# Attention output summed with `o` as the moving operand and turned by VectorE, FFN weights w1 and w3 as moving operand: a decode kernel before and after

## The chip, the cores and the metric

The kernel runs on one core of one Trainium2 chip. The metric is the device time of one execution in microseconds (us). The profile's span is some 2 us shorter than the time (2.6 us in the kernel before), since it goes from the first to the last instruction. Ratios are the mean time of one kernel's fast runs over the mean of the other's fast runs of the same rounds, with a 95% interval, so they are not quite the ratio of the medians that stand beside them. In the profile lines PE is TensorE and PEld its weight loads, DVE is VectorE, ACT ScalarE, POOL GpSimd and SP the engine whose queue issues the loads.

## The reference, cut to what matters

One decode step of four sequences: layer norm of x, attention of 32 heads over the last 2048 positions of the cache, a SwiGLU FFN on the same normalised x, and the residual.

```python
# x: (4, 1, 640); k_cache, v_cache: (4, 32, 8192, 192); all bf16
xn = layernorm(x)
q = xn @ wq                                     # 32 heads of 192
k, v = k_cache[:, :, -2048:, :], v_cache[:, :, -2048:, :]
p = softmax(q @ k^T * 192 ** -0.5)
attn = (p @ v).reshape(B, 1, 32 * 192) @ wo
ffn = (silu(xn @ w1) * (xn @ w3)) @ w2          # 640 -> 1536 -> 640
return x + attn + ffn
```

K and V of the window are 3 MB each for every head, so 201 of the 223 MB that are loaded.

## The kernel before: what the change and the argument touch

A head's K and V each come in one transfer with one contiguous row of 24,576 bytes for each of the 128 partitions. The tile pools stand one behind another in a partition: constants first, then FFN weights, K (2 buffers), V (3), products, wo, small tiles.

```python
const = ctx.enter_context(tc.tile_pool(name="const", bufs=1))
fpool = ctx.enter_context(tc.tile_pool(name="ffn", bufs=1))
kpool = ctx.enter_context(tc.tile_pool(name="kt", bufs=KBUFS))
vpool = ctx.enter_context(tc.tile_pool(name="vt", bufs=VBUFS))
ppool = ctx.enter_context(tc.tile_pool(name="pr", bufs=PBUFS))
# ... wopool, small, PSUM pools ...

def load_k(h):
    kt = kpool.tile([P, NJ, Dh], BF16, tag="kt")
    nc.sync.dma_start(out=kt[:].rearrange("q j d -> q (j d)"),
                      in_=k_win[:, h].rearrange("b (p j) d -> p b (j d)", p=PB))
```

Scores: VectorE multiplies K with q (`mult`, four quarters a head), TensorE adds up groups of columns (`adder`), VectorE reduces. P·V leaves two halves (even and odd positions) in one PSUM tile. They are merged, turned and normalised head by head. (In `nc.tensor.matmul`, `lhsT` is called the stationary operand and `rhs` the moving one.)

```python
# pv(h), after its 32 matmuls: ScalarE masks the odd half
nc.scalar.activation(out=o_odd[:], in_=o_ps[:, Dh:2 * Dh], func=ACTF.Copy, scale=half[:, 1:2])
# pv_merge(h): VectorE adds the even half
nc.vector.scalar_tensor_tensor(out=o_raw[:], in0=o_banks[h % 2][:, 0:Dh], scalar=half[:, 0:1],
                               in1=o_odds.pop(h)[:], op0=ALU.mult, op1=ALU.add)
# ge_tr(h): six small matmuls with o as the stationary operand
for i in range(RPP):
    nc.tensor.matmul(gp[sl, i, :], lhsT=o_raw[:, i:Dh:RPP], rhs=sel[:], start=True, stop=True)
# ge_copy(h): times 1 / sum, into oT, which ge_proj multiplies with wo
# ffn_in: 60 matmuls a weight, each with a 128x128 block of it as the stationary operand
nc.tensor.matmul(ffn["ps"][:, c, :], lhsT=ffn[name][:, kc, c:F:FC], rhs=xnT[:, kc, 0, :], ...)
```

The loads run over one queue. The last ones are V of the last three heads, most of w2, the last wo, and two small pieces of w2.

## Time and profile before

| | before |
|---|---|
| time, median (range) of 3 runs | 530.63 us (529.79 to 531.39) |
| span of the profiled run | 527.5 us |
| load queue, share of 16 transfer engines | 98.7% |
| steady stretch, 60 to 480 us | 431 GB/s |
| VectorE / TensorE busy | 69% / 66% |

A reading of the page begins with the shares. Where the transfers are busy in every slice and no engine comes near that (69% at most here), an engine's busy time is not the bound. The next question is at which moments the transfers were *not* running at their rate. For that, busy time by stretch is the view. The lines themselves are in the prediction below.

### The profile page before, as it was taken

What the parts mean: (1) busy time and instruction counts of PE and PEld (TensorE: products, weight loads), DVE (VectorE), ACT (ScalarE), POOL (GpSimd) and SP (SyncE); (2) the same over time, 40 slices, a digit from 0 to 9 for tenths busy, and PEclk for the clock granted to TensorE, in tenths of its full rate; (3) what the DMA queues carried; (4) which work ended last, traced back from release to release, by engine and by line L of the source; (5) the groups of instructions that cost most, each with busy time, mean ns of one, the idle gap of its engine ahead of it and who ended that gap; (6) DMA issues with size and microseconds to landing.
All of it is one profiled execution on the core that took longest, in us unless ns stands there. A gap on an engine that the chain in (4) does not pass through costs nothing.

```text
span 527.5 us, 6169 instructions
## 1 busy us (share of the span) xinstructions
PE 350.7 (66%) x2642; PEld 163.0 (31%) x2643; DVE 362.9 (69%) x505; ACT 43.7 (8%) x144; POOL 1.1 (0%) x8
## 2 busy tenths in 40 slices
PE   2765866666856867666768765566676676656775
PEld 0322332332523433232323332232332332323333
DVE  3179885777558478686757887577768766777961
ACT  2111000000101000000000000000000000000010
POOL 0000000000000000000000000000000000000000
PEclk9989897988968797787887899799898977998987
DMA  8999999999999999999999999999999999999995
GB/s 358 432 432 415 418 439 436 421 442 422 430 440 425 434 426 435 432 432 432 432 431 432 430 429 436 426 436 428 430 435 429 435 429 435 429 434 419 434 429 216
DMA packets 11570, 223.35 MB, mean 423 GB/s; under 512 B 1292, under 2 KB 1304, under 8 KB 2584
## 3 DMA queue, kind: packets, MB, share of 16 engines
q1 hardware_dynamic: 11528, 222.96, 98.7%
q8 instruction: 20, 0.33, 0.2%
q14 instruction: 6, 0.05, 0.0%
q10 hardware_dynamic: 16, 0.01, 0.0%
HBM read 222.96 MB, written 0.01 MB: 423 GB/s over the span
## 4 chain that ended last, share of the span: by engine, by line
DMA 63%; DVE 20%; PE 13%; ACT 2%; issue 1%; SPq 0%
DMA kt<-in_A_k_cache_dram 49%; DVE pr L204 14%; PE ps L215 9%; DMA w<-in_B_w_dram 7%; DMA wo_t<-in_A_wo_dram 4%; DMA wt<-in_A_wq_dram 4%; DVE sc L223 3%; PE qps L172 1%; PE gp L301 1%; DVE z L259 1%; ACT ex L251 1%; PE mt L245 1%; PE o_ps L267 1%; ACT L251 0%; DVE o_raw L279 0%
## 5 line engine op out<-in xcount | busy, mean ns | idle before, releaser
L215 PE MATMUL ps<-pr,idb 128*128 128x512 bf16 x768 | 222.3, 433 | 152.6 <-DVE pr L204 152.4
L204 DVE TENSOR_TENSOR pr<-kt,qbc 128x3072 bf16<-128x3072 bf16 x128 | 224.0, 1751 | 102.0 <-DMA kt<-in_A_k_cache_dram 101.7
L215 PEld LDWEIGHTS <-idb 128*128 128x128 bf16 x768 | 78.5, 106 | 248.2 <-issue 195.6
L223 DVE TENSOR_REDUCE sc<-ps 128x16 f32<-128x512 f32 x128 | 87.4, 683 | 3.2 <-PE ps L215 2.2
L267 PE MATMUL o_ps<-vt,z 128*8 128x384 bf16 x1024 | 55.9, 355 | 1.4 <-DMA vt<-in_A_v_cache_dram 1.4
L267 PEld LDWEIGHTS <-z 128*8 128x8 bf16 x1024 | 25.2, 90 | 28.0 <-issue 17.0
L301 PEld LDWEIGHTS gp<-sel,o_raw 128*32 128x32 f32 x384 | 24.7, 151 | 16.4 <-issue 9.8
L274 ACT ACTIVATE o_odd<-o_ps,half 128x192 f32<-128x192 f32 x32 | 13.5, 421 | 189.4 <-PE o_ps L267 187.5
L301 PE MATMUL gp<-sel,o_raw 128*32 128x4 f32 x384 | 27.3, 200 | 0.8 <-DVE o_raw L279 0.8
L248 ACT COPY negm<-mt 128x1 f32<-128x1 f32 x32 | 5.1, 159 | 258.8 <-PE mt L245 258.8
L259 DVE TENSOR_TENSOR z<-ex,mask_b 128x256 bf16<-128x256 bf16 x32 | 13.5, 422 | 14.3 <-ACT ex L251 13.9
L172 PE MATMUL qps<-wt,xnT 128*128 128x512 bf16 x59 | 16.1, 429 | 5.3 <-DMA wt<-in_A_wq_dram 5.2
L279 DVE SCALAR_TENSOR_TENSOR o_raw<-o_ps,half,o_odd 128x192 f32<-128x192 f32 x32 | 13.1, 409 | 6.6 <-ACT o_odd L274 6.6
L178 DVE CAST qbc<-qps 128x512 bf16<-128x512 f32 x6 | 3.8, 685 | 18.2 <-PE qps L172 18.2
L245 PEld LDWEIGHTS mt<-ones_ff,gneg 1*128 1x128 f32 x64 | 10.2, 198 | 15.8 <-issue 14.4
L245 PE MATMUL mt<-ones_ff,gneg 1*128 1x1 f32 x64 | 12.9, 268 | 0.6 <-DVE gneg L240 0.6
L232 PE MATMUL mt<-idf,lmax 128*1 128x128 f32 x32 | 11.4, 357 | 1.1 <-DVE lmax L227 1.1
L251 ACT ACTIVATE ex<-sc,negm 128x64 bf16<-128x64 f32 x32 | 11.1, 348 | 1.0
L172 PEld LDWEIGHTS <-xnT 128*128 128x128 bf16 x60 | 6.4, 107 | 14.6 <-issue 8.7
L193 PE MATMUL acc<-wo_t,oT 128*4 128x320 bf16 x96 | 9.8, 308 | 0.4 <-DMA wo_t<-in_A_wo_dram 0.4
L237 DVE TENSOR_REDUCE gmax<-mt 1x4 f32<-1x128 f32 x32 | 8.8, 275 | 1.3 <-PE mt L232 0.8
L286 PEld LDWEIGHTS mt<-mask_f,rsum 128*32 128x32 f32 x64 | 4.6, 109 | 14.0 <-issue 12.5
(52 smaller groups left out, 84.2 us busy)
## 6 DMA issues: line engine op xcount, KB each, us to landing
kt<-in_A_k_cache_dram SPq DMA_DIRECT2D x32, 3072.0 KB, 19.8
vt<-in_A_v_cache_dram SPq DMA_DIRECT2D x32, 3072.0 KB, 27.4
wo_t<-in_A_wo_dram SPq DMA_DIRECT2D x8, 960.0 KB, 22.9
wt<-in_A_wq_dram SPq DMA_DIRECT2D x2, 3072.0 KB
w<-in_B_w_dram SPq DMA_DIRECT2D x2, 1920.0 KB, 24.3
wt<-in_A_wq_dram SPq DMA_DIRECT2D x1, 1536.0 KB, 19.9
w<-in_B_w_dram SPq DMA_DIRECT2D x1, 1280.0 KB, 34.9
w<-in_B_w_dram SPq DMA_DIRECT2D x2, 320.0 KB, 36.8
```

Of the source, the lines that this page charges most:

```text
L172: nc.tensor.matmul(qp[:], lhsT=xnT[:, kc].rearrange("p a b -> p (a b)"), rhs=wq_rows[kc][:, (c0 + i) * QC:(c0 + i + 1) * QC], start=(kc == ...
L204: nc.vector.tensor_tensor(out=pr[:], in0=kts[h][:, g * JQ:(g + 1) * JQ, :], in1=qbc[:, h * Dh:(h + 1) * Dh].unsqueeze(1).to_broadcast([P, ...
L215: nc.tensor.matmul(ps[:], lhsT=idb[:], rhs=pr[:, :, kk * DD:(kk + 1) * DD], start=(kk == 0), stop=(kk == NK - 1))
L223: nc.vector.tensor_reduce(out=scs[h][:, g * JQ:(g + 1) * JQ], in_=pss.pop(u)[:], axis=AX.X, op=ALU.add)
L232: nc.tensor.transpose(out=mt[0:1, 0:P], in_=chs[h][0][:], identity=idf[:])
L245: nc.tensor.matmul(mt[:, P:P + 1], lhsT=gneg[:].rearrange("o p b -> o (p b)"), rhs=ones_ff[0:1, 0:1], start=True, stop=True)
L251: nc.scalar.activation(out=ex[:], in_=scs.pop(h)[:], func=ACTF.Exp, bias=negm[:, 0:1], scale=SCALE, accum_out=rsum[:])
L259: nc.vector.tensor_tensor(out=z[:], in0=ex[:].unsqueeze(2).to_broadcast([P, NJ, B]), in1=mask_b[:].unsqueeze(1).to_broadcast([P, NJ, B]), ...
L267: nc.tensor.matmul(o_ps[c * CT:c * CT + 2 * B, :], lhsT=z[:, 2 * jj:2 * jj + 2, :], rhs=vt[:, 2 * jj:2 * jj + 2, :], start=(jj < 4), stop= ...
L274: nc.scalar.activation(out=o_odd[:], in_=o_ps[:, Dh:2 * Dh], func=ACTF.Copy, scale=half[:, 1:2])
L279: nc.vector.scalar_tensor_tensor(out=o_raw[:], in0=o_banks[h % 2][:, 0:Dh], scalar=half[:, 0:1], in1=o_odds.pop(h)[:], op0=ALU.mult, op1=A ...
L301: nc.tensor.matmul(gp[sl, i, :], lhsT=o_raw[:, i:Dh:RPP], rhs=sel[:], start=True, stop=True)
```

## The change

The intent is to take small instructions off TensorE and VectorE. `o` and the FFN weights w1 and w3 become the moving operand, and the normalising and the turn to columns are done once per four heads instead of once per head, with a VectorE transpose of 32x32 blocks. The residual is loaded a second time, later, so that its matmuls can come later; the final copy becomes one. The cut below leaves out that the FFN's product is now also turned on VectorE (one 128x384 pass into `hb` and one transpose), that the softmax sums land in `po`, and that the sums of heads 29 and 30 come one or two slots earlier.

```diff
-        nc.scalar.activation(out=o_odd[:], in_=o_ps[:, Dh:2 * Dh], func=ACTF.Copy, scale=half[:, 1:2])
+        o_sb = small.tile([P, 2 * Dh], FP32, tag="o_sb", bufs=2, name="o_sb")
+        nc.scalar.copy(out=o_sb[:], in_=o_ps[:])
 ...
-        nc.vector.scalar_tensor_tensor(out=o_raw[:], ...)          # pv_merge, every head
-        nc.vector.reciprocal(out=rtb[sl, :], ...)                   # ge_norm, every head
-        for i in range(RPP):                                        # ge_tr, every head
-            nc.tensor.matmul(gp[sl, i, :], lhsT=o_raw[:, i:Dh:RPP], rhs=sel[:], start=True, stop=True)
-        nc.vector.tensor_tensor(out=oTs[hg][sl], ...)               # ge_copy, every head
+        for par in range(2):                                        # ge_sum, every head
+            nc.tensor.matmul(po[sl, 0:Dh], lhsT=sel_w[:, par].rearrange("p a b -> p (a b)"),
+                             rhs=o_sb[:, par * Dh:(par + 1) * Dh], start=(par == 0), stop=(par == 1))
+        nc.vector.reciprocal(out=rt[:], in_=po[:, Dh:Dh + 1])       # ge_rec, every four heads
+        og = small.tile([P, RPP, CT], BF16, tag="og", bufs=1, name="og")   # ge_turn, every four heads
+        nc.vector.tensor_scalar_mul(out=og[:].rearrange("p i r -> p r i"),
+                                    in0=po[:, 0:Dh].rearrange("p (r i) -> p r i", i=RPP), scalar1=rts.pop(hg)[:, 0:1])
+        oT = small.tile([P, RPP, CT], BF16, tag="oT", bufs=2, name="oT")
+        nc.vector.transpose(out=oT[:].rearrange("p i r -> p (i r)"), in_=og[:].rearrange("p i r -> p (i r)"))
 ...
-    half, sel = const.tile([P, 2], FP32), const.tile([P, B], FP32)          # shortened
-    sT, hT = const.tile([P, FC, B], FP32), const.tile([P, FC, B], BF16)     # shortened
+    tot_w, sel_w = const.tile([P, NREP, B], FP32), const.tile([P, 2, NREP, B], FP32)   # shortened
+    sT = const.tile([P, FW], FP32, name="sT")
+    hb = const.tile([P, FC, CT], BF16, name="hb")
+    hT = const.tile([P, FC, CT], BF16, name="hT")
 ...
+        xr["t"] = const.tile([B, D], BF16, name="x_res")
+        nc.sync.dma_start(out=xr["t"][:], in_=A_x.rearrange("b s d -> (b s) d"))
 ...
-                nc.tensor.matmul(ffn["ps"][:, c, :], lhsT=ffn[name][:, kc, c:F:FC], rhs=xnT[:, kc, 0, :], ...)
+                nc.tensor.matmul(ffn["ps"][w * CT:(w + 1) * CT, :], lhsT=xnT[:, kc].rearrange("p a b -> p (a b)")[:, 0:CT],
+                                 rhs=ffn[name][:, kc, w * FW:(w + 1) * FW], ...)
 ...
-    nc.vector.tensor_copy(out=res[:, 0:NH], in_=acc[0:NR, 0:NH])
-    nc.scalar.copy(out=res[:, NH:N0], in_=acc[0:NR, NH:N0])
+    nc.vector.tensor_copy(out=res[:], in_=acc[0:NR, :])
```

More of the change, by code (lines that the diff above doesn't have):

```diff
@@ L64 @@
     assert JQ * DD == 512 and JQ % 2 == 0 and 2 * Dh <= 512 and 2 * N0 == D and N0 <= 512
-    assert (H * Dh) % QC == 0 and NQ % 6 == 0 and QW % P == 0 and Dh % RPP == 0 and P == HG * CT
+    assert (H * Dh) % QC == 0 and NQ % 6 == 0 and QW % P == 0 and Dh == CT * RPP and P == HG * CT and F == HG * CT * FC
     assert 2 * H * Dh <= NJ * Dh and KBUFS == 2 and VBUFS == 3
@@ L79 @@
     ps_t = ctx.enter_context(tc.tile_pool(name="ps_t", bufs=1, space=MemoryType.PSUM))
+    ps_po = ctx.enter_context(tc.tile_pool(name="ps_po", bufs=1, space=MemoryType.PSUM))
     ps_acc = ctx.enter_context(tc.tile_pool(name="ps_acc", bufs=1, space=MemoryType.PSUM))
@@ L85 @@
     kts, vts, prs, pss, scs, exs, zs = {}, {}, {}, {}, {}, {}, {}
-    wos, o_odds, o_raws, rsums, rtbs, chs, ges, oTs = {}, {}, {}, {}, {}, {}, {}, {}
+    wos, o_sbs, rsums, rts, chs, oTs = {}, {}, {}, {}, {}, {}
     def load_k(h):
@@ L132 @@
                             axis=AX.X, op=ALU.add)
-    half = const.tile([P, 2], FP32, name="half")
-    nc.vector.tensor_reduce(out=half[:], in_=rows[:].rearrange("q (two b) -> q two b", b=B), axis=AX.X, op=ALU.add)
-    sel = const.tile([P, B], FP32, name="sel")
-    nc.vector.tensor_tensor(out=sel[:], in0=rows[:, 0:B], in1=rows[:, B:2 * B], op=ALU.add)
+    NREP = CT // B
+    tot_w = const.tile([P, NREP, B], FP32, name="tot_w")
+    nc.vector.tensor_copy(out=tot_w[:], in_=mask_f[:].unsqueeze(1).to_broadcast([P, NREP, B]))
+    sel_w = const.tile([P, 2, NREP, B], FP32, name="sel_w")
+    for par in range(2):
+        nc.vector.tensor_copy(out=sel_w[:, par], in_=rows[:, par * B:(par + 1) * B].unsqueeze(1).to_broadcast([P, NREP, B]))
     xf = ppool.tile([B, D], FP32, tag="pr")
@@ L197, in acc_add, with x_load, x_add @@
             acc_half(i, lhsT, rhs, last=last)
-    acc_half(0, idb[0:B, 0:B], x_sb, first=True)
+    po = ps_po.tile([P, Dh + 1], FP32, name="po")
+    xr = {}
+    def x_load():
+        xr["t"] = const.tile([B, D], BF16, name="x_res")
+        nc.sync.dma_start(out=xr["t"][:], in_=A_x.rearrange("b s d -> (b s) d"))
+    def x_add(i):
+        acc_half(i, idb[0:B, 0:B], xr["t"], first=True)
     def mult(u):
@@ L230, in chain_tr @@
     def chain_tr(h):
-        mt = ps_m.tile([P, P + 1 + B], FP32, tag="mt")
+        mt = ps_m.tile([P, P + 1], FP32, tag="mt")
         nc.tensor.transpose(out=mt[0:1, 0:P], in_=chs[h][0][:], identity=idf[:])
@@ L272, in pv @@
         vts.pop(h)
-        o_odd = small.tile([P, Dh], FP32, tag="o_odd", bufs=2, name="o_odd")
-        nc.scalar.activation(out=o_odd[:], in_=o_ps[:, Dh:2 * Dh], func=ACTF.Copy, scale=half[:, 1:2])
-        o_odds[h] = o_odd
-    def pv_merge(h):
-        o_raw = small.tile([P, Dh], FP32, tag="o_raw", bufs=2, name="o_raw")
-        nc.vector.scalar_tensor_tensor(out=o_raw[:], in0=o_banks[h % 2][:, 0:Dh], scalar=half[:, 0:1],
-                                       in1=o_odds.pop(h)[:], op0=ALU.mult, op1=ALU.add)
-        o_raws[h] = o_raw
+        o_sb = small.tile([P, 2 * Dh], FP32, tag="o_sb", bufs=2, name="o_sb")
@@ L284, in ge_tot @@
+        nc.scalar.copy(out=o_sb[:], in_=o_ps[:])
+        o_sbs[h] = o_sb
     def ge_tot(h):
         sl = slice((h % HG) * CT, (h % HG + 1) * CT)
-        nc.tensor.matmul(chs[h][1][sl, P + 1:P + 1 + B], lhsT=rsums.pop(h)[:].to_broadcast([P, CT]), rhs=mask_f[:],
+        nc.tensor.matmul(po[sl, Dh:Dh + 1], lhsT=tot_w[:].rearrange("p a b -> p (a b)"), rhs=rsums.pop(h)[:],
                          start=True, stop=True)
-    def ge_norm(h):
-        sl = slice((h % HG) * CT, (h % HG + 1) * CT)
-        rtb = small.tile([P, B], FP32, tag="rtb")
-        nc.vector.reciprocal(out=rtb[sl, :], in_=chs.pop(h)[1][sl, P + 1:P + 1 + B])
-        rtbs[h] = rtb
@@ L295, in ge_tr @@
-    def ge_tr(h):
-        hl = h % HG
-        sl = slice(hl * CT, (hl + 1) * CT)
-        gp = ps_t.tile([P, RPP, B], FP32, tag="t", name="gp")
-        o_raw = o_raws.pop(h)
-        for i in range(RPP):
-            nc.tensor.matmul(gp[sl, i, :], lhsT=o_raw[:, i:Dh:RPP], rhs=sel[:], start=True, stop=True)
-        ges[h] = gp
-    def ge_copy(h):
-        hg, hl = h // HG, h % HG
-        sl = slice(hl * CT, (hl + 1) * CT)
-        if hl == 0:
-            oTs[hg] = small.tile([P, RPP, B], BF16, tag="oT", bufs=2, name="oT")
-        nc.vector.tensor_tensor(out=oTs[hg][sl], in0=ges.pop(h)[sl, :, :],
-                                in1=rtbs.pop(h)[sl, :].unsqueeze(1).to_broadcast([CT, RPP, B]), op=ALU.mult)
+        chs.pop(h)
@@ new lines, in ge_rec, with ge_sum @@
+    def ge_rec(hg):
+        rt = small.tile([P, 1], FP32, tag="rt", bufs=2, name="rt")
+        nc.vector.reciprocal(out=rt[:], in_=po[:, Dh:Dh + 1])
+        rts[hg] = rt
+    def ge_sum(h):
+        sl = slice((h % HG) * CT, (h % HG + 1) * CT)
+        o_sb = o_sbs.pop(h)
+        for par in range(2):
+            nc.tensor.matmul(po[sl, 0:Dh], lhsT=sel_w[:, par].rearrange("p a b -> p (a b)"),
+                             rhs=o_sb[:, par * Dh:(par + 1) * Dh], start=(par == 0), stop=(par == 1))
@@ L312, in ge_proj, with ge_turn @@
+    def ge_turn(hg):
+        og = small.tile([P, RPP, CT], BF16, tag="og", bufs=1, name="og")
[3 more added lines that the diff above has]
+        nc.vector.transpose(out=oT[:].rearrange("p i r -> p (i r)"), in_=og[:].rearrange("p i r -> p (i r)"))
+        oTs[hg] = oT
     def ge_proj(hg, i0, i1):
@@ L314, in ge_proj @@
         for i in range(i0, i1):
-            acc_add(oT[:, i, :], wo_t[:, i * D:(i + 1) * D])
-    sT = const.tile([P, FC, B], FP32, name="sT")
-    hT = const.tile([P, FC, B], BF16, name="hT")
+            acc_add(oT[:, i, 0:B], wo_t[:, i * D:(i + 1) * D])
+    FW = F // HG
+    sT = const.tile([P, FW], FP32, name="sT")
+    hb = const.tile([P, FC, CT], BF16, name="hb")
+    hT = const.tile([P, FC, CT], BF16, name="hT")
     ffn = {}
@@ L325, in ffn_load, with ffn_in @@
         ffn[name] = wt
-    def ffn_in(name, c0, c1):
-        if c0 == 0:
-            ffn["ps"] = ps_t.tile([P, FC, B], FP32, tag="t", name="f_ps")
-        for c in range(c0, c1):
-            for kc in range(KC):
-                nc.tensor.matmul(ffn["ps"][:, c, :], lhsT=ffn[name][:, kc, c:F:FC], rhs=xnT[:, kc, 0, :],
-                                 start=(kc == 0), stop=(kc == KC - 1))
+    def ffn_in(name):
+        ffn["ps"] = ps_t.tile([P, FW], FP32, tag="t", name="f_ps")
+        for kc in range(KC):
+            for w in range(HG):
+                nc.tensor.matmul(ffn["ps"][w * CT:(w + 1) * CT, :], lhsT=xnT[:, kc].rearrange("p a b -> p (a b)")[:, 0:CT],
+                                 rhs=ffn[name][:, kc, w * FW:(w + 1) * FW], start=(kc == 0), stop=(kc == KC - 1))
     def ffn_silu():
@@ L338, in ffn_h @@
     def ffn_h():
-        nc.vector.tensor_tensor(out=hT[:], in0=ffn.pop("ps")[:], in1=sT[:], op=ALU.mult)
+        nc.vector.tensor_tensor(out=hb[:].rearrange("p c r -> p r c"),
+                                in0=ffn.pop("ps")[:].rearrange("p (r c) -> p r c", c=FC),
+                                in1=sT[:].rearrange("p (r c) -> p r c", c=FC), op=ALU.mult)
+        nc.vector.transpose(out=hT[:].rearrange("p c r -> p (c r)"), in_=hb[:].rearrange("p c r -> p (c r)"))
     w2_v = B_w2.rearrange("(p c) n -> p c n", c=FC)
@@ L352, in ffn_out @@
         for c in range(*W2C[i:i + 2]):
-            acc_add(hT[:, c, :], ffn["w2"][:, c, :], last=(c == FC - 1))
+            acc_add(hT[:, c, 0:B], ffn["w2"][:, c, :], last=(c == FC - 1))
     sched = defaultdict(list)
@@ L358, in add @@
         sched[slot].append((phase, len(sched[slot]), fn, args))
-    ends = {H - 3: (NU - 1, NU + 3), H - 2: (NU + 2, NU + 4), H - 1: (NU + 6, NU + 7)}
+    ends = {H - 3: (NU - 1, NU + 1), H - 2: (NU + 2, NU + 3), H - 1: (NU + 6, NU + 7)}
     for h in range(H):
@@ L378 @@
         add(ul + 4, 5, ge_tot, h)
-        add(ul + 4, 9, ge_norm, h)
+        if h % HG == HG - 1:
+            add(ul + 4, 9, ge_rec, h // HG)
         v, m = ends.get(h, (u0 + L, u0 + L + 1))
         add(v, 7, pv, h)
-        add(m, 0, pv_merge, h)
-        add(m, 7, ge_tr, h)
-        add(m + 1, 0, ge_copy, h)
+        add(m, 7, ge_sum, h)
+        if h % HG == HG - 1:
+            add(m + 1, 0, ge_turn, h // HG)
     e = ends[H - 1][1] + 1
@@ L392 @@
     add(f, 0, ffn_load, "w1", B_w1)
-    add(f + 7, 7, ffn_in, "w1", 0, FC)
+    add(f + 7, 7, ffn_in, "w1")
     add(f + 7, 9, ffn_silu)
     add(f + 8, 0, ffn_load, "w3", B_w3)
-    add(f + 15, 7, ffn_in, "w3", 0, FC)
+    add(f + 15, 7, ffn_in, "w3")
     add(f + 15, 9, ffn_h)
-    add(1, 6, acc_half, 1, idb[0:B, 0:B], x_sb, True)
+    add(8, 0, x_load)
+    add(16, 6, x_add, 0)
+    add(17, 6, x_add, 1)
     add((H - 3) * GQ + 1, 0, wo_load, NG - 2)
@@ L417 @@
             fn(*args)
-    NR, NH = CT + B, N0 // 2
+    NR = CT + B
     res = ppool.tile([NR, N0], BF16, tag="pr", name="res")
-    nc.vector.tensor_copy(out=res[:, 0:NH], in_=acc[0:NR, 0:NH])
-    nc.scalar.copy(out=res[:, NH:N0], in_=acc[0:NR, NH:N0])
+    nc.vector.tensor_copy(out=res[:], in_=acc[0:NR, :])
     out_v = out.rearrange("b s d -> (b s) d")
```

## The prediction

> **What bounds the kernel now.** I read the busy line first, then the forty slices, then the queues and the share of the chain that ended last.
>
> ```profile
> PE 350.7 (66%) x2642; PEld 163.0 (31%) x2643; DVE 362.9 (69%) x505; ACT 43.7 (8%) x144; POOL 1.1 (0%) x8
> ...
> DMA  8999999999999999999999999999999999999995
> GB/s 358 432 432 415 418 439 436 421 442 422 430 440 425 434 426 435 432 432 432 432 431 432 430 429 436 426 436 428 430 435 429 435 429 435 429 434 419 434 429 216
> ...
> q1 hardware_dynamic: 11528, 222.96, 98.7%
> ...
> DMA 63%; DVE 20%; PE 13%; ACT 2%; issue 1%; SPq 0%
> ```
>
> No compute engine is above 69%, while the one load queue keeps the 16 transfer engines busy for 98.7% of the span, and every slice but the first and the last reads 9. The kernel is a stream of 222.96 MB, almost all K and V. The chain gives VectorE 20% and TensorE 13%, but the chain names what releases the next *issue* on the queue; it does not say that the engines moving data stood still. So I asked for busy time by stretch (columns: stretch and its length, busy time and count of each engine, clock, DMA share, GB/s):
>
> ```profile
> 2.00:524.00 522.00, 350.32 (x2640) 162.99 (x2643) 362.29 (x503) 42.80 (x143) 0.00 (x0) 0.88 1.00 427
> 5.00:510.00 505.00, 340.05 (x2502) 156.79 (x2503) 356.85 (x485) 40.61 (x137) 0.00 (x0) 0.88 1.00 431
> 520.00:524.00 4.00, 3.21 (x46) 2.17 (x47) 0.60 (x2) 0.30 (x1) 0.00 (x0) 0.84 0.38 154
> ...
> 42.00:44.00 2.00, 1.19 (x7) 0.48 (x5) 2.00 (x2) 0.00 (x0) 0.00 (x0) 1.00 0.86 258
> ```
>
> For 505 us the rate is 431 GB/s; the only hole I found is at 42 to 44 us (258 GB/s, so about 0.8 us lost at 430), where the queue waits for the first K buffer to come free. From about 485 us the queue waits for nothing: all last loads are issued by 488.2 us and need until 523.95. The end itself (columns: start, duration, what):
>
> ```profile
> 487.85 36.06 DMA w<-in_B_w_dram
> 523.90 0.04 issue
> 523.95 0.45 PE acc L193 x4
> 524.40 0.02 issue
> 524.42 0.33 DVE res L421
> 524.75 0.02 issue
> 524.77 0.29 ACT res L422
> ```
>
> The last piece of w2 lands, four matmuls and two copies follow, then the output goes out. Compute can shorten the time only before about 5 us, in the 0.8 us hole, or after 523.95.
>
> [...] this change adds 5 KB. [...] about 5 KB / 431 GB/s = 0.01 us. [...]
>
> **The change part by part.** These rows go (line, engine, operation, shapes, count, busy us, mean ns):
>
> ```profile
> L301 PE MATMUL gp<-sel,o_raw 128*32 128x4 f32 x384 | 27.3, 200 | 0.8 <-DVE o_raw L279 0.8
> L274 ACT ACTIVATE o_odd<-o_ps,half 128x192 f32<-128x192 f32 x32 | 13.5, 421 | 189.4 <-PE o_ps L267 187.5
> L279 DVE SCALAR_TENSOR_TENSOR o_raw<-o_ps,half,o_odd 128x192 f32<-128x192 f32 x32 | 13.1, 409 | 6.6 <-ACT o_odd L274 6.6
> L292 DVE RECIPROCAL rtb<-mt 32x4 f32<-32x4 f32 x32 | 5.6, 176 | 1.9 <-PE mt L286 1.2
> L309 DVE TENSOR_TENSOR oT<-gp,rtb 32x24 bf16<-32x24 f32 x32 | 5.6, 176 | 3.0 <-PE gp L301 2.7
> ```
>
> VectorE loses 13.1 + 5.6 + 5.6 = 24.3 us. It gains, once per four heads, a reciprocal (0.18), a normalising pass over 128x192 from PSUM (like o_raw, 0.41) and a 128x192 bf16 transpose[...]. Eight times 0.97 is 7.8 us. Net about -16.5 us, to 346 us.
> ScalarE copies 384 columns instead of 192. Slope from 421 ns at 192 to the 594 ns cast at 512: 0.54 ns a column, so 0.52 us, 32 times +0.1 = +3 us.
> TensorE: 12 records a head become four of 192 columns (an f32 matmul of this program is two records: 384 = 32 x 6 x 2). The 120 FFN matmuls of 4 columns, each with a 128x128 weight load, become 40 of 384 columns in four column groups. I expect 10 to 20 us less busy time, but leave this rough, since TensorE waits 152.4 us for the products anyway.
> All of it lies beside the transfers. In the steady stretch VectorE already sits idle 101.7 us for K; it will sit idle about 118. The hole at 42 us follows from the first four products, which the change does not touch; the load of x is issued later.
>
> The path that can move is **the tail**. Before: the last P·V ends at 519.8, the first w2 piece's 16 matmuls and the 12 small ones end near 522.05, oT is ready at 522.28, its projection starts at 522.43 with the last wo, and all is done at 524.40. After: the same 16 matmuls end near 521.8 (estimate); two f32 matmuls of 192 columns take 0.6 to 0.9 us (estimate from the 128-column f32 record's 270 ns against 200 ns for 4 columns, and a granted clock of 0.50 from 517 to 520); then 0.41 + 0.38 and two hand-overs of 0.05. So oT is ready near 523.5, 1.2 us later. The projection's 12 and the last 8 matmuls took 0.98 + about 0.5 us when ready, so the sums end near 525.1: +0.7. Then one 36x320 cast, 317 + 160 x 1.05 = 0.48 us, replaces 0.33 + 0.02 + 0.29: -0.15. **Sum: +0.55 us, so about 531.2 us** on the median of 530.63.
>
> **The rivals.** (a) *Faster because engines are relieved.* 16 us of VectorE and the small matmuls in the chain's list speak for it. [...] It could take at most the 0.8 us hole and some of the shortfall between 427 and 431: at best 528.5. (b) *The shared PSUM tile `po` becomes a wait.* The first head of each next group writes its sum into `po` after the old group is normalised. By the schedule, normalising stands in slot 22 and the next write to the tile in slot 23 (counted in quarter heads from the group's start), so the order fits; if it stalled TensorE, K has about 3.5 us of queued data (a head's 6.29 MB lasts 14.6 us, four products' slots take about 11). Nothing until then; at worst +3 us. (c) *The tail costs more,* if the clock stays at 0.50: the f32 pair doubles, +0.7 us more, 531.9. (d) *The residual's load is late* and holds TensorE: it is issued near 53 us, needed eight slots later, and loads land in about 23 us. I expect no wait.
>
> **Range and chances.** Three runs before lie between 529.79 and 531.39, so scatter is ±0.8 us. The tail gives 0 to +1.2, the stream perhaps -1 to +0.5. Central 531.1, range 529.6 to 532.6. 2% is 10.6 us: [...] a loss needs an unseen stall in each group. Same: 0.98.
>
> **What would show it right or wrong.** Right: slices of the transfers still 9, queue near 98.7%, VectorE near 346 us with its wait for K up by about 15 us, span within 2 us; last w2 landing near 524; oT after it or close to it; sums ending 0.3 to 1.2 us later after that landing than the 0.45 us here. Wrong: slices of 8 or less in the middle, a TensorE wait on the normalising, the transpose or x_res of more than 1 us each, or a transpose far above 0.4 us.

The 0.38 us for the transpose (part of the 0.97, and in 0.41 + 0.38) rests on no trace of this case; in the changed kernel it took 378 ns (L311 of its page). The 1.05 ns a column of the last cast is the slope, in the kernel before, between the 36x160 cast, 317 ns, and the 128x512 cast, 685 ns. That no rate above 431 GB/s can be had, as the 528.5 of rival (a) assumes, was not shown either: from 60 to 480 us these runs reach 431 or 432 at most.

## The result, and the profile after

The changed kernel takes 533.78 us (median of 4 runs, 532.4 to 534.3) against 530.39 (4 runs). The ratio is 1.0058 [1.0032, 1.0084], some 3.1 us longer: inside 2%, but above the predicted range.

The same lines of the page of the changed kernel (busy by engine, transfers in forty slices, the load queue, the chain):

```profile
PE 342.7 (65%) x2306; PEld 144.5 (27%) x2307; DVE 350.2 (66%) x435; ACT 45.6 (9%) x143; POOL 1.1 (0%) x8
...
DMA  8999999999999999999999999999999999999995
GB/s 356 445 417 422 417 435 434 426 434 422 431 434 421 433 423 433 430 426 433 426 423 437 424 428 429 428 432 424 428 429 432 427 432 426 432 427 406 428 427 220
...
q1 hardware_dynamic: 11536, 222.97, 98.6%
...
DMA 60%; DVE 23%; PE 15%; ACT 1%; issue 1%; SPq 0%
```

VectorE has 12.7 us less to do, TensorE 8 us less. The queue is as full as before (98.6%, the slices still read 9), with the same bytes. Yet 15 of the 40 slices read 430 or more, where 24 did before. The steady stretch says it in one number. First the kernel before, then the changed one (stretch, length, busy time and count of PE, weight loads, VectorE, ScalarE and GpSimd, clock, transfer share, GB/s):

```profile
60.00:480.00 420.00, 282.96 (x2175) 132.65 (x2173) 302.21 (x412) 30.95 (x114) 0.00 (x0) 0.87 1.00 431
```

```profile
60.00:480.00 420.00, 274.71 (x1866) 114.66 (x1865) 285.70 (x345) 31.59 (x108) 0.00 (x0) 0.88 1.00 429
```

The share is 1.00 in both: the transfer engines did not stand idle for a late buffer, so the pieces took a little longer. Over 420 us, 2 GB/s of 431 are about 2 us, and the whole stream is 520 us long. V of the last head, for which the last P·V waits, lands at 519.79 instead of 517.10 us, so 2.7 of the 3.0 us of span are lost before the tail begins.

The tail, in the chain that ended last of the changed kernel (start, duration, what):

```profile
524.34 1.08 DVE og L308
525.42 0.02 issue
525.44 0.39 DVE oT L311
525.83 0.04 issue
525.87 1.54 PE acc L196 x20
527.41 0.02 issue
527.44 0.48 DVE res L430
```

Nothing here waits for a transfer any more: the chain runs over the normalising pass and the transpose. From the moment at which the first w2 piece lets its matmuls begin to the issue of the output it is 522.91 to 527.95, 5.04 us; before, 520.15 to 525.09, 4.94 us. The tail costs 0.1 us in this pair of profiles.

The new groups that carry it (line, engine, operation, shapes, count, busy us, mean ns, idle before):

```profile
L303 PE MATMUL po<-o_sb,sel_w 128*32 128x192 f32 x128 | 35.0, 409 | 0.5 <-ACT o_sb L285 0.5
L285 ACT COPY o_sb<-o_ps 128x384 f32<-128x384 f32 x32 | 15.3, 479 | 193.6 <-PE o_ps L278 193.6
L308 DVE TENSOR_SCALAR og<-po,rt 128x192 bf16<-128x192 f32 x8 | 8.4, 1055 | 8.0 <-PE po L303 8.0
L311 DVE STREAM_TRANSPOSE oT<-og 128x192 bf16<-128x192 bf16 x8 | 3.0, 378 | 0.3
```

So two things called for a cause: a stream that is 0.5% slower with the same bytes and no gap, and a normalising pass of 1,055 ns where 410 were expected.

### The profile page after: what moved, and what is told of

Read it like the earlier page. It is cut to its first block, busy times and chain, and to the rows that moved or that the text cites.

```text
span 530.5 us, 5427 instructions
## 1 busy us (share of the span) xinstructions
PE 342.7 (65%) x2306; PEld 144.5 (27%) x2307; DVE 350.2 (66%) x435; ACT 45.6 (9%) x143; POOL 1.1 (0%) x8
## 3 DMA queue, kind: packets, MB, share of 16 engines
q1 hardware_dynamic: 11536, 222.97, 98.6%
## 4 chain that ended last, share of the span: by engine, by line
DMA 60%; DVE 23%; PE 15%; ACT 1%; issue 1%; SPq 0%
DMA kt<-in_A_k_cache_dram 50%; DVE pr L215 15%; PE ps L226 8%; DMA w<-in_B_w_dram 6%; DVE sc L234 4%; DMA wt<-in_A_wq_dram 3%; PE qps L175 2%; PE po L303 2%; DVE og L308 1%; DVE z L270 1%; PE o_ps L278 1%; ACT ex L262 1%; PE acc L196 1%; DVE oT L311 1%; ACT L262 0%
## 5 line engine op out<-in xcount | busy, mean ns | idle before, releaser
L226 PE MATMUL ps<-pr,idb 128*128 128x512 bf16 x768 | 212.5, 418 | 161.8 <-DVE pr L215 161.8
L215 DVE TENSOR_TENSOR pr<-kt,qbc 128x3072 bf16<-128x3072 bf16 x128 | 223.3, 1745 | 110.6 <-DMA kt<-in_A_k_cache_dram 110.6
L226 PEld LDWEIGHTS <-idb 128*128 128x128 bf16 x768 | 76.2, 103 | 262.8 <-issue 206.4
L303 PE MATMUL po<-o_sb,sel_w 128*32 128x192 f32 x128 | 35.0, 409 | 0.5 <-ACT o_sb L285 0.5
L285 ACT COPY o_sb<-o_ps 128x384 f32<-128x384 f32 x32 | 15.3, 479 | 193.6 <-PE o_ps L278 193.6
L303 PEld LDWEIGHTS po<-o_sb,sel_w 128*32 128x32 f32 x128 | 13.8, 130 | 20.9 <-issue 14.5
L308 DVE TENSOR_SCALAR og<-po,rt 128x192 bf16<-128x192 f32 x8 | 8.4, 1055 | 8.0 <-PE po L303 8.0
L290 PEld LDWEIGHTS po<-rsum,tot_w 128*32 128x32 f32 x64 | 4.7, 112 | 14.7 <-issue 13.1
```

Of the source, the lines that this page charges most:

```text
L215: nc.vector.tensor_tensor(out=pr[:], in0=kts[h][:, g * JQ:(g + 1) * JQ, :], in1=qbc[:, h * Dh:(h + 1) * Dh].unsqueeze(1).to_broadcast([P, ...
L226: nc.tensor.matmul(ps[:], lhsT=idb[:], rhs=pr[:, :, kk * DD:(kk + 1) * DD], start=(kk == 0), stop=(kk == NK - 1))
L285: nc.scalar.copy(out=o_sb[:], in_=o_ps[:])
L303: nc.tensor.matmul(po[sl, 0:Dh], lhsT=sel_w[:, par].rearrange("p a b -> p (a b)"), rhs=o_sb[:, par * Dh:(par + 1) * Dh], start=(par == 0), ...
L308: nc.vector.tensor_scalar_mul(out=og[:].rearrange("p i r -> p r i"), in0=po[:, 0:Dh].rearrange("p (r i) -> p r i", i=RPP), scalar1=rts.pop ...
```

## The experiments

**Where the buffers start.** The engines' work did not explain a slower transfer without a gap, so I read the placement of the buffers from the two built programs (bytes from the start of a partition):

```
                 constants end   first K buffer             first V buffer
before                  34,560   49,920  = 195 x 256         99,072 = 387 x 256
changed                 38,944   54,304  = 212 x 256 + 32   103,456 = 404 x 256 + 32
```

The constants of the changed kernel are 4,384 bytes larger: x_res 1,280, sT 1,344, hb 768, hT 672, and tot_w with sel_w in place of half with sel 320 (half and sel with 32 bytes each: only so do the parts add up to the 4,384). 4,384 is 17 x 256 + 32. Every big buffer begins 32 bytes past a multiple of 256. That is theory A. Theory B is the natural rival: wider f32 copies and f32 sums that get in the transfers' way. Theory C is the small load of x in the middle of the stream.

In what follows "steady" is the rate from 60 to 480 us. Each run had its own runs of the kernel before on the same chip: 529.89 us for the first four experiments, 530.57 for the next four, 529.76 for the last four.

### b_p288: only the placement of the changed kernel

```diff
     hT = const.tile([P, FC, B], BF16, name="hT")
+    pad = const.tile([P, 72], FP32, name="pad")     # never used
```

> The kernel before with one unused constant of 288 bytes a partition behind the others: no instruction changes, only where the big buffers start (K, V, weights: 0 bytes past a multiple of 64 before; 32 bytes past one here, as in the changed kernel). Theory A (the stream is slower because its destinations start off alignment): 2 to 3 us slower than before, rate in the steady stretch 428 to 429 GB/s instead of 431. Theory B (the stream is slower because of what the engines do beside it: wider f32 copies, the f32 sums): the time of before within 0.7 us, 431 GB/s.

Measured: 534.50 us against 529.89, ratio 1.0087 [1.0069, 1.0105].

```profile
60.00:480.00 420.00, 274.25 (x2150) 129.22 (x2150) 297.91 (x407) 30.36 (x111) 0.00 (x0) 0.89 1.00 429
40.00:46.00 6.00, 4.04 (x17) 1.65 (x16) 5.53 (x6) 0.00 (x0) 0.00 (x0) 0.95 0.64 238
```

Not one instruction differs from before, and the steady rate is 429. Theory A gets its slowdown; theory B did not allow one. The time is even longer than in the changed kernel, 4.6 us over before where 2 to 3 were expected. The second line shows why that may be: the hole after the start, where the queue waits for a K buffer, is deep in this profile (238 GB/s from 40 to 46 us, transfer share 0.64). I come back to it below.

### a_p224: the changed kernel with the old placement

```diff
     hT = const.tile([P, FC, CT], BF16, name="hT")
+    pad = const.tile([P, 56], FP32, name="pad")     # never used
```

> The changed kernel with one unused constant of 224 bytes a partition, which puts the big buffers 256 bytes past a multiple of 512, as in the kernel before. Theory A: 2 to 3 us faster than the changed kernel, so within about 1 us of before (about +0.5 us, the tail), 431 GB/s. Theory B: the changed kernel's time again, about 3 us over before, 428 to 429 GB/s.

Measured: 530.22 us against 529.89, ratio 1.0008 [0.9990, 1.0027].

```profile
60.00:480.00 420.00, 272.95 (x1881) 115.07 (x1880) 290.68 (x351) 32.77 (x114) 0.00 (x0) 0.89 1.01 432
```

With all of the change's work and none of its misplacement the rate is back (432) and the kernel is not distinguishable from before. These two runs, taken together, settle the main point: placement alone makes the loss, and placement alone takes it away.

### b_p512: moved, with the alignment kept

The pad is 128 elements of 4 bytes, 512 bytes.

> Control: the kernel before, big buffers moved by 512 bytes a partition, so moved but with the alignment kept. Theory A and theory B: the time of before within 0.7 us. If it is 2 us slower, moving itself or the place matters, not the 32 bytes.

Measured: 530.37 us against 529.89, ratio 1.0009 [0.9992, 1.0026]. Moving by itself costs nothing that these runs can see.

### a_nox: without the second load of x

```diff
-        xr["t"] = const.tile([B, D], BF16, name="x_res")
-        nc.sync.dma_start(out=xr["t"][:], in_=A_x.rearrange("b s d -> (b s) d"))
+        xr["keep"] = const.tile([B, D], BF16, name="x_res")
+        xr["t"] = x_sb
```

> The changed kernel with the second load of x taken out: the residual is added from the tile loaded at the start; the place of the unused tile is kept, so addresses are those of the changed kernel. Theory A and B: no change from the changed kernel (about +3 us over before). Theory C (the small four-row transfer in the middle of the stream costs the time): 2 to 3 us faster than the changed kernel.

Measured: 533.05 us against 529.89, ratio 1.0067 [1.0049, 1.0084]: as slow as the changed kernel. Theory C falls.

### b_p32, b_p64, b_p128, b_p256: which boundary

The kernel before, with pads of 32, 64, 128 and 256 bytes. The big buffers start at a multiple of 32, 64, 128 and 512.

> The kernel before, big buffers 32 bytes further (288 past a multiple of 512). Theory A (start off a multiple of 64 bytes slows the transfers), as the 288-byte shift showed it: +3 to +4.5 us, 428 to 429 GB/s in the steady stretch. If the place within 512 matters and not the 32 bytes: the time of before.

> The kernel before, big buffers 64 bytes further (a multiple of 64, not of 128 or 256). If 64 bytes is the boundary that matters: the time of before within 0.7 us. If the boundary is 128 or 256 bytes (before, they start at a multiple of 256): +3 us or more, as with 32.

> The kernel before, big buffers 128 bytes further (a multiple of 128, not of 256). Boundary of 64 or 128: the time of before within 0.7 us. Boundary of 256: +3 us.

> The kernel before, big buffers 256 bytes further: they start at a multiple of 512, where before they start 256 past one. If a multiple of 256 is what the transfers want: the time of before within 0.7 us and 431 GB/s. If just the place 256 past a multiple of 512 is good (or this kernel's own layout): +2 to +3 us and 429 GB/s.

| kernel | big buffers start at a multiple of | median, us | before, us | ratio [95%] | steady, GB/s |
|---|---|---|---|---|---|
| b_p32 | 32 | 533.61 | 530.57 | 1.0052 [1.0027, 1.0077] | 429 |
| b_p64 | 64 | 532.65 | 530.57 | 1.0039 [1.0010, 1.0067] | 429 |
| b_p128 | 128 | 533.03 | 530.57 | 1.0046 [1.0019, 1.0073] | 429 |
| b_p256 | 512 | 529.92 | 529.76 | 1.0001 [0.9974, 1.0028] | 431 |
| b_p512 | 256 | 530.37 | 529.89 | 1.0009 [0.9992, 1.0026] | 431 |

The boundary is 256 bytes in these runs: 431 GB/s where the big buffers start at a multiple of 256 or 512, 429 where they do not. How far past it a buffer starts (32, 64 or 128 bytes) makes no difference that these runs resolve: the three intervals overlap, and the losses of 2.1 to 2.8 us are a little below the 3 us that the expectations named. I had let 64 bytes be the first guess in two of the expectations; that guess is wrong.

The runs show that moving the destination alone brings the loss: the source was never moved.

### b_pr32: only what is behind the K and V buffers

```diff
+    padp = ctx.enter_context(tc.tile_pool(name="padp", bufs=1))      # between vpool and ppool
     ppool = ctx.enter_context(tc.tile_pool(name="pr", bufs=PBUFS))
 ...
+    pad = padp.tile([P, 8], FP32, name="pad")                        # 32 bytes
```

> The kernel before with only what stands behind the K and V buffers moved by 32 bytes: product tiles, wo tiles and the small tiles that VectorE, TensorE and ScalarE read and write; wq, K, V and the FFN weights (215 of 223 MB) keep their alignment. Theory A1 (the transfers' own writes are slower off alignment): the time of before, at most +0.2 us for the 7.9 MB of wo. Theory A2 (the engines' accesses off alignment disturb the transfers or slow the engines): +3 us.

Measured: 529.63 us against 530.57, ratio 0.9989 [0.9960, 1.0018], steady rate 431 GB/s. The tiles that the engines write are off the boundary here as in b_p32, and nothing happens; so it is where wq, K, V and the FFN weights land that matters. Whether the engines' *reading* of a K or V tile off the boundary has a part in it this run cannot tell; the transfer share of 1.00 at a lower rate (429 GB/s in b_p32) speaks for the transfers' own pieces, and so does the next pair.

### b_s4 and b_s4_p32: a cost per piece or per byte

```diff
-        nc.sync.dma_start(out=kt[:].rearrange("q j d -> q (j d)"), in_=...)
+        JS = NJ // 4
+        for s in range(4):
+            nc.sync.dma_start(out=kt[:, s * JS:(s + 1) * JS, :].rearrange("q j d -> q (j d)"),
+                              in_=k_rows[:, :, s * JS * Dh:(s + 1) * JS * Dh])      # V likewise
```

> The kernel before with each K and V load cut into four (6,144 bytes a partition in place of 24,576), alignment kept. It is the control of the next run. All theories: the time of before or up to 6 us over, if shorter pieces cost something by themselves.

> The same cut into four, big buffers moved by 32 bytes. Theory P (a fixed cost per piece that starts off alignment, one piece a partition and load): four times the pieces, so four times the +2.5 to +3 us: +9 to +12 us over the run b_s4. Theory Q (every byte written off alignment is a little slower, however it is cut): +2.5 to +3.5 us over the run b_s4.

Measured: b_s4 539.46 us, ratio 1.0183 [1.0158, 1.0207]; b_s4_p32 551.43 us, ratio 1.0395 [1.0369, 1.0422], both against 529.76. The cut alone costs 9.7 us, more than the up to 6 us expected; for 1,536 more pieces an engine that is about 6 ns each (an estimate from this time and the counts below; the 16 packets under 512 bytes that come with each further load are in it). The 32 bytes cost 11.3 us by the means here (12.0 by the medians), 3.6 times the 3.1 us by which the uncut loads were slower on average (below). First the steady stretch of b_s4, then that of b_s4_p32:

```profile
60.00:480.00 420.00, 280.87 (x2161) 130.48 (x2160) 298.23 (x407) 30.13 (x110) 0.00 (x0) 0.87 1.02 424
```

```profile
60.00:480.00 420.00, 275.78 (x2099) 127.87 (x2099) 291.59 (x396) 29.67 (x109) 0.00 (x0) 0.87 1.02 416
```

The transfers are as full as can be and yet slower, twice: once for being cut, once for the 32 bytes. Theory P holds, a fixed cost for each piece that starts off the boundary: there are 3.4 times as many pieces. The engines read the same tiles at the same places in both pairs, so their reading off the boundary cannot account for the larger loss. The cost can be sized. The queue has 39,176 packets in b_s4 and 11,528 in the kernel before, so 144 for each of the 192 further loads: 128 pieces, one a partition, and 16 packets under 512 bytes (4,364 of these over all queues, against 1,292). Uncut, there are 80 loads of 128 pieces, 640 for each of the 16 engines if they are spread evenly; the six kernels with misplaced buffers and uncut loads (the changed one, a_nox, b_p288, b_p32, b_p64, b_p128) have a mean ratio of 1.0058, 3.1 us, so 4.8 ns a piece. Cut, there are 272 loads, 2,176 pieces for each engine, and 11.3 us make 5.2 ns a piece. (Both are estimates from these times and counts.) A cost per byte would have been the same 3 us in both.

### a_best: alignment, a pass that writes without a stride, and the hole

```diff
+    pad = const.tile([P, 56], FP32, name="pad")
 ...
-        nc.vector.tensor_scalar_mul(out=og[:].rearrange("p i r -> p r i"),
-                                    in0=po[:, 0:Dh].rearrange("p (r i) -> p r i", i=RPP), scalar1=rts.pop(hg)[:, 0:1])
+        nc.vector.tensor_scalar_mul(out=og[:], in0=po[:, 0:Dh].rearrange("p (r i) -> p i r", i=RPP),
+                                    scalar1=rts.pop(hg)[:, 0:1])
 ...
     for h in range(KBUFS):
         load_k(h)
+    wo_load(0)                                       # not in slot 8
```

> The changed kernel with alignment restored (224 bytes), the normalising pass reading PSUM with a stride and writing without one, and the first wo load (960 KB, 2.2 us at 431 GB/s) issued at the start so that it fills the hole near 42 us. The normalising pass: 0.4 us instead of 1.05, the tail 0.6 us shorter; the hole 0.5 to 1.5 us smaller. Sum: 0.5 to 1.5 us faster than before, 529 us against 530, unless something else is hit.

Measured: 529.08 us (528.53 to 529.68) against 529.76, ratio 0.9982 [0.9962, 1.0002]. The point estimate is 1 us better than before, but the interval just reaches 1, so it is not shown to beat it. It is the best of the variants of the changed kernel. The three parts of the edit were not timed one by one, but the trace shows each at work: first the normalising group, then the end of the chain, then the stretch of the hole.

```profile
L309 DVE TENSOR_SCALAR og<-po,rt 128x192 bf16<-128x192 f32 x8 | 3.3, 407 | 9.6 <-PE po L304 9.6
```

```profile
523.07 0.46 PE acc L197 x4
523.52 0.02 issue
523.54 0.48 DVE res L433
```

```profile
40.00:46.00 6.00, 3.35 (x16) 1.30 (x15) 5.96 (x7) 0.00 (x0) 0.00 (x0) 1.00 1.00 430
```

The pass takes 407 ns with a contiguous write and a read step of 24 bytes in PSUM, instead of 1,055 ns with a write step of 64 bytes; the sums again end with the four matmuls that wait for the last piece of w2; the hole is closed.

**The hole and the scatter.** In the kernel before, and in all the others with uncut loads but a_best, the queue runs short at 40 to 46 us, when it waits for the first K buffer to come free. Its depth differs between profiles, and goes roughly with the clock that TensorE was granted from 30 to 40 us, when the first products are summed (352 to 410 GB/s at 0.83, 221 to 344 at 0.66 to 0.71; within the two groups it does not follow the clock):

| profiled run | clock, 30 to 40 us | GB/s, 40 to 46 us |
|---|---|---|
| b_p512 | 0.83 | 410 |
| after | 0.83 | 406 |
| before | 0.83 | 401 |
| b_pr32 | 0.83 | 393 |
| a_nox | 0.83 | 373 |
| b_p64 | 0.83 | 352 |
| b_p128 | 0.71 | 221 |
| b_p256 | 0.70 | 253 |
| b_p288 | 0.69 | 238 |
| a_p224 | 0.66 | 344 |
| b_p32 | 0.66 | 332 |

A rate of 240 instead of 431 GB/s over 6 us is 2.7 us. This is likely one reason why single runs of one kernel differ by up to 4.5 us (529.05 to 533.50 for the kernel before), and may be why b_p288 came out 1.5 to 2 us above b_p32. But it was only seen in one profile each, and no run set the clock; it is not shown.

The same traces show a second place where time is lost, the tail. From the first w2 piece to the issue of the output, b_p256, which has the instructions of the kernel before, takes 6.21 us in its profile at a granted clock of 0.50, and b_p512 4.99 at 0.76. The profile of a_nox, whose tail is that of the changed kernel, takes 7.47 us at 0.50, and the changed kernel 5.04 at 1.00. That run of a_nox is its slowest (535.11 us, the other five are at most 533.21), though its hole is shallow (373 GB/s).

The steady rates, 431 or 432 with aligned buffers and 429 without in all eleven, do not go with the clock.

## Why the prediction was wrong, point by point

- **The bound was right.** The kernel is bound by the stream before and after; every slice of the transfers but the ends reads 9, and the queue share is 98.6%. Work on the engines bought nothing, as rival (a) was judged. (The hole near 42 us was read too large: the stretches beside the one of 258 GB/s read 467 and 479, and over 40 to 46 us the rate is 401, so some 0.4 us are lost and not 0.8.)
- **The step that failed is the term for the stream**, "the stream perhaps -1 to +0.5". It rested on the words "this change adds 5 KB" and "about 5 KB / 431 GB/s = 0.01 us": the prediction treated the rate as fixed by the bytes. It looked at the change for what it moves *in time* and never for where it moves the *buffers*. The runs put +2.7 us there (the span lost before the tail begins; 3.1 us is the whole difference), over five times the upper end of that term, and none of the four rivals named it. What stands in place of the failed step is a fixed cost of some 5 ns (estimate above) for each piece whose destination starts off a multiple of 256 bytes; a_p224 takes the loss away without touching the work. That a larger constant shifts everything behind it could have been read from the diff and the two built programs.
- **The tail was mis-sized in two terms that nearly cancel, and came out too large.** Predicted +0.7 for the sums and -0.15 for the final copy; measured +0.1 together. The f32 sums cost less here: they and the 16 w2 matmuls end 1.40 us after the first w2 piece (522.91 to 524.31), where some 2.4 were predicted. That estimate had taken up the clock of 0.50 that was granted just before; here it was 1.00. In the profile of a_nox the same matmuls ran at 0.50 and took 2.53 us, so the clock was guessed wrong and not the work. First the changed kernel, then a_nox (columns as above):

```profile
522.91:524.31 1.40, 1.39 (x20) 0.82 (x19) 0.00 (x0) 0.14 (x1) 0.00 (x0) 1.00 0.73 282
```

```profile
523.33:525.86 2.53, 2.52 (x20) 1.22 (x19) 0.00 (x0) 0.14 (x1) 0.00 (x0) 0.50 0.46 169
```

The normalising pass cost more: 1,055 ns where 0.41 us had been taken from the old merging pass of the same size. That pass wrote without a stride, and this one writes with a step of 64 bytes. a_best takes the stride away and has 407 ns. The transpose was right (0.378 against 0.38), and so was the final copy (0.48).

- **With the alignment restored the predicted total holds, in part by luck.** a_p224 is 1.0008 of before, +0.4 us with an interval from -0.5 to +1.4; predicted was +0.55. The interval takes in 0, and two terms behind the +0.55 were off and nearly cancel, so the agreement does not confirm the working.
- **Engines.** VectorE was to fall to 346 us; it is at 350.2. The 8 normalising passes take 5.1 us more than they would at 407 ns, and the FFN's new pass and transpose on VectorE, 1.9 and 0.6 us, were not counted at all. TensorE fell by 8 us, predicted 10 to 20, and mostly not for the reason given: the new sums are busy for 35.0 us where the small matmuls that they replace took 27.3, the FFN's for 3.5 instead of 7.4, and the fall stands in the adding matmuls (212.5 us, 222.3 before), which the change does not touch. ScalarE rose by 1.9, predicted 3. VectorE's wait for K was to rise from 101.7 to some 118 us; it is 110.6 (these are waits of the whole span, not of the steady stretch as the prediction has it). None of this is on the path.
- **Rivals (b) and (d)** did not happen. The trace of the changed kernel lists no wait for x_res and none of the matmuls into the shared tile for the normalising pass; only three weight loads of the softmax maximum (`mt`) wait for it, at most 0.4 us each, 1.3 us in all. **Rival (c)**, a tail made longer by a low clock, is not in the profile of the changed kernel, whose clock was 1.00 from the first w2 piece on. It is in that of a_nox: 7.47 us at 0.50. The 20 matmuls of sums and first w2 piece took 2.53 us there against 1.40 at 1.00, so 1.8 times as long. Against the old tail at 0.50 (6.21 us in b_p256) the whole is 1.3 us more, where the pair at a high clock differs by 0.1. So the tail's cost depends on the clock that a run happens to get; it is read from one profile each.

## What to carry to other kernels

When a kernel is bound by transfers, check where their destinations start: here a 32-byte step past a multiple of 256 cost 0.6% with pieces of 24 KB, and 2% with pieces of 6 KB. A diff that adds or resizes small tiles ahead of the big ones can do this silently; compare buffer addresses as well as instructions, and pad to 256 (tested here) or put the big buffers first (not tested). If the rate falls while the transfer share stays at its full value (429 for 431 GB/s at a share of 1.00 here), look at the pieces and not at the waits.
